# One reciprocal per pair in place of eight, four small GpSimd copies, and a new written order of the work

## The chip, the cores and the metric

The kernel runs on one core of a Trainium2 chip. A core has five engines with queues of their own: TensorE (PE in the profile, with its weight loads listed apart as PEld), VectorE (DVE), ScalarE (ACT), GpSimd (POOL) and SyncE (SP), which here issues all DMAs. PE writes only into PSUM; the other engines work on SBUF and, but for GpSimd, on PSUM too. The metric is the device time of one execution in microseconds, the median of several.

## The reference

Soft-capped attention over 8 batches, 12 heads, 448 positions and a head width of 64, followed by a feed-forward part whose gate comes from a causal convolution of 5 taps:

```python
scores = scale * np.matmul(q, k.transpose(0, 1, 3, 2))
scores = cap * np.tanh(scores / cap)
scores = scores - np.max(scores, axis=-1, keepdims=True)
attn = np.exp(scores)
attn = attn / (np.sum(attn, axis=-1, keepdims=True) + 1e-09)
attn_out = np.matmul(attn, v)                      # then (B, S, H * D), 768 wide
gate_pre += conv_w[k][None, None, :] * xp[:, k:k + S, :]   # for each of 5 taps
gate = 1.0 / (1.0 + np.exp(-gate_pre))
val = x @ w_val
return (gate * val @ w_out).astype(np.float32)
```

The step that the change touches is the division by the sum of each row of `attn`.

## The kernel before, in words

Two heads make a pair; there are 48 pairs, six to a batch. The 128 partitions hold the two heads' 64 channels each, as four groups of 32 partitions (`GROUPS`): groups 0 and 1 belong to the first head, groups 2 and 3 to the second. For a pair:

- SP loads q, k (four DMAs each) and v (two DMAs). DVE turns q and k in 32x32 blocks (L448). From pair 13 on, both are also cut into a high part (ACT, L454) and a low part (DVE, L383), and the scores are three products in place of one.
- PE makes the scores in four chunks of 112 keys (`scores`, L469) into one of two PSUM tiles (`pss`). ACT applies tanh (L477) and exp (L481) to each chunk (`pt`). DVE adds chunks together ahead of the row sums (`add`, L488 and L491): none for the first six pairs, all four into one from pair 11 on.
- PE multiplies `pt` with v into `psa` (`av`, L507) and with ones into `psz` (`sums`, L523). There is one buffer of each; the odd ones of the first six pairs use tiles named `psf` instead.
- Now the division. The sums of 448 rows are spread over the two groups of a head, 224 to a group. `turn_sums` (L529, DVE) turns them so that each partition has 7 sums, `norm_recip` adds the guard (L536) and takes reciprocals (L540), `spread` (L546, DVE) turns them back, now broadcast over 32 channels, and `norm_mul` (L554, DVE) multiplies `psa` by them into `u`. Every group needs the reciprocals of both halves of its head: its own 7 columns and those of the neighbour group. So L540 writes `rc`, 14 columns wide, with eight instructions of 32 partitions by 7 elements, half of which read from the neighbour's partitions.
- `u` is cut into `xh` (ACT, L559) and `xl` (DVE, L383) for the value projection, and DVE makes the convolution from it (L573, L575; the first tap of the first 11 pairs on ACT, L571).

For a batch, once its six pairs are there: ACT's sigmoid on the gates (L581), PE's value projection in halves of three channel blocks (`val`, L596 to L598, three products each), DVE's product with the gate (`gate`, L602), a high and a low part (`gated_hi` L605 on ACT, `gated_lo` L383 on DVE), PE's output projection in halves (`out_part`, L625 to L627), a copy out of PSUM (`store`, L633, ACT) and the DMA out (`store_out`, L637, SP). 448 is three and a half times 128, so every second batch leaves 64 rows to the next one: `keep_tail` (L612) moves them on GpSimd, twice for each of four batches. It is all that GpSimd does after the start. The two weight matrices are loaded and cut into high and low parts in twelve steps early on (L279 to L290), the convolution's weights once (`load_conv_w`; L300 loads, L311 to L314 prepare).

The order is written out by hand, as numbers. `PAIRS` has a row for each pair and in it a time for each step named in `STEPS`, counted in pairs and relative to the pair's own number; `BLOCKS` has a row for each batch, `WEIGHTS` for each weight step, and `CW_LOAD`, `CW_AT` and `W_FREE` place three single steps. All steps are sorted by these times and issued in that order under a manual schedule, so that each engine's queue, SP's and POOL's too, runs its instructions in exactly that order. An instruction whose input isn't there holds up all that stands behind it on its engine.

Of the kernel before, what the change touches and what calls it, by code (L numbers as in the profile page):

```python
# [7 lines left out]
F32 = mybir.dt.float32  # L8
# [34 lines left out]
    "add add add av av av av sums sums sums sums turn_sums recip spread mul x_hi x_lo conv conv conv conv conv"  # L43
).split()
PAIRS = """
- - -3.064 -9.09 -5.622 - - - - -4.262 -5.451 -4.05 -3.713 -3.983 -4.666 -3.924 -3.438 -3.329 -3.464 -3.153 -1.811 - -
  - -2.746 -2.598 -1.455 -0.365 -2.81 -1.83 -1.743 -1.539 -1.354 -1.021 0.536 0.696 1.014 3.151 1.192 1.24 1.616 1.869
  2.29
-5.242 -4.446 -1.697 -5.062 -4.398 - - - - -4.347 -4.229 -2.87 -2.909 -4.283 -3.621 -2.153 -2.144 -2.433 -1.59 -0.767
  -1.588 - - - -1.585 -1.248 -0.673 -0.458 -2.299 -1.473 0.346 0.383 0.475 0.582 0.646 0.669 2.05 2.71 1.397 2.009  # L50
  2.138 2.228 2.305
-4.37 -4.577 -1.599 -3.197 -3.579 - - - - -2.956 -1.738 -1.485 -0.821 -2.404 -1.055 -0.603 -0.573 -1.126 -0.649 -0.165
  -0.246 - - - -0.498 -0.333 0.44 0.542 -1.035 -0.323 -0.032 0.045 0.622 0.651 0.927 1.346 2.559 2.796 1.643 2.115
  2.477 2.536 2.862
-3.867 -3.827 -0.48 -3.708 -2.408 - - - - -1.417 -1.284 -1.129 -0.899 -1.259 -1.006 -0.603 -0.517 -0.987 -0.577 -0.121
  0.182 - - - -0.092 0.457 0.74 0.839 -0.67 -0.089 0.042 0.439 0.522 0.625 0.709 1.033 2.962 3.062 1.339 1.695 1.805
  2.076 2.385
-2.147 -3.045 -0.082 -1.922 -2.656 - - - - -1.37 -0.682 -0.02 -0.433 -0.576 -0.258 0.044 -0.177 -0.16 -0.144 0.242
  0.055 - - - 0.076 0.114 0.466 0.498 0.048 0.332 0.425 0.434 0.742 0.82 0.952 1.348 2.039 2.351 1.815 2.116 2.374
  2.436 2.515  # L60
-3.132 -2.604 -0.301 -2.118 -1.544 - - - - -0.68 -1.014 -0.654 -0.433 -0.544 -0.823 -0.138 0.222 -0.286 -0.093 0.036
  0.269 - - - 0.255 0.453 0.668 0.75 -0.24 0.21 0.414 0.553 0.669 0.722 0.984 1.101 1.256 1.566 1.471 1.551 2.023
  2.457 2.71
-2.592 -2.549 -0.928 -1.311 -1.58 - - - - -0.222 -0.561 -0.183 -0.988 -0.182 -0.397 -0.049 -0.65 0.08 0.167 0.202
  0.211 0.4 0.521 - 0.179 0.224 0.335 0.872 0.799 0.872 - - 1.024 1.233 1.519 1.751 3.543 3.796 2.13 2.869 3.058 3.256
  3.886
-2.49 -2.096 -0.928 -1.564 -1.888 - - - - -0.119 -0.898 -0.11 -0.988 0.3 -0.435 0.536 -0.422 0.429 0.505 0.667 0.745
  1.102 1.056 - 0.977 1.043 1.054 1.08 1.147 1.202 - - 1.219 1.38 1.485 1.753 2.392 3.921 3.14 3.64 3.787 3.931 3.989
-1.946 -2.927 -0.201 -1.477 -0.909 - - - - -0.199 -0.174 0.359 0.264 -0.126 0.044 0.638 0.423 0.708 0.35 0.717 0.797
  0.977 1.023 - 0.829 0.854 1.048 1.269 1.087 1.236 - - 1.679 1.752 1.784 1.986 2.393 3.269 2.657 3.368 3.424 3.498  # L70
  3.653
-2.393 -2.701 0.359 -1.57 -0.973 - - - - -0.338 -0.119 -0.33 0.024 -0.277 0.072 -0.018 0.087 0.751 0.714 0.556 0.552
  1.063 1.24 - 1.227 1.274 1.404 1.425 1.191 1.395 - - 1.65 1.803 1.982 2.063 2.96 3.19 2.44 3.241 3.241 3.314 3.627
-2.751 -1.165 0.435 -1.245 -0.761 - - - - -0.701 0.069 -0.683 0.143 -0.014 0.329 -0.498 0.452 0.245 0.622 0.789 0.934
  0.958 1.087 - 1.201 1.226 1.26 1.341 1.097 1.272 - - 1.329 1.533 1.662 1.704 2.377 2.856 2.579 2.733 2.863 2.916
  3.42
-1.653 -2.409 -0.503 -1.187 -1.793 - - - - 0.056 -0.489 -0.487 0.07 0.532 -0.335 -0.192 0.27 0.641 0.818 -0.083 0.684
  1.055 0.816 1.111 0.78 0.867 1.056 1.058 1.114 - - - 1.202 1.273 1.71 1.757 1.778 1.858 2.275 2.63 2.65 3.045 3.412
-1.985 -2.388 -0.519 -0.474 -0.538 - - - - -0.444 -0.458 0.268 0.163 -0.013 -0.095 0.589 0.356 0.179 0.681 0.882 0.927
  1.039 1.099 1.326 1.055 1.366 1.425 1.426 1.507 - - - 1.517 1.633 1.782 1.782 2.76 3.615 1.902 2.302 2.801 2.812  # L80
  3.214
-3.454 -1.521 0.862 -1.941 -0.941 -1.662 -0.798 -0.758 -0.355 0.036 0.039 0.529 0.517 0.293 0.286 0.589 0.573 0.359
  0.306 0.619 0.752 0.577 0.79 0.852 1.078 1.094 1.161 1.481 1.255 - - - 1.375 1.407 1.527 1.762 2.714 2.89 2.216
  2.427 2.707 3.284 3.378
# [36 lines left out]
-2.966 -2.807 0.096 -2.131 -1.597 -0.618 -1.292 -0.287 -0.879 -0.107 -0.061 0.233 0.37 -0.039 0.069 0.627 0.493 0.099
  0.33 0.636 0.502 0.408 0.71 0.809 0.909 0.986 1.146 1.366 0.819 - - - 1.134 1.166 1.458 1.653 2.3 2.369 2.503 2.552
# [739 lines left out]
```

## Time and profile before

| | |
|---|---|
| median of 3 runs | 733.51 us (733.31 to 734.77) |
| profiled execution | 733.1 us |
| its span, first to last instruction | 731.2 us |
| PE busy | 699.2 us (96%) |
| DVE busy | 622.2 us (85%) |
| ACT busy | 593.3 us (81%) |
| POOL busy | 7.1 us (1%) |
| mean granted TensorE clock | 0.997 |

How to read the rows that follow. A group of instructions is "line engine operation out<-in, shapes, xcount | busy us, mean ns of one | us that its engine idled ahead of it, and what ended the idle time". A row of waits is "engine tile line <- what it waited for: us in all, times, longest". A row of a timeline is "start us, us, engine line operation out<-in, xcount", with idle time ahead and what ended it in brackets; neighbouring instructions of one kind are merged into a row. A row of stages is "from:to, length, busy us of each engine, granted clock (1.00 is full), share of the DMA engines, GB/s".

### The profile page before, as it was taken

What the parts mean: (1) busy time and instruction counts of PE and PEld (TensorE: products, weight loads), DVE (VectorE), ACT (ScalarE), POOL (GpSimd) and SP (SyncE); (2) the same over time, 40 slices, a digit from 0 to 9 for tenths busy, and PEclk for the clock granted to TensorE, in tenths of its full rate; (3) what the DMA queues carried; (4) which work ended last, traced back from release to release, by engine and by line L of the source; (5) the groups of instructions that cost most, each with busy time, mean ns of one, the idle gap of its engine ahead of it and who ended that gap; (6) DMA issues with size and microseconds to landing.
All of it is one profiled execution on the core that took longest, in us unless ns stands there. A gap on an engine that the chain in (4) does not pass through costs nothing.

```text
span 731.2 us, 13364 instructions
## 1 busy us (share of the span) xinstructions
PE 699.2 (96%) x5024; PEld 480.1 (66%) x5024; DVE 622.2 (85%) x1308; ACT 593.3 (81%) x750; POOL 7.1 (1%) x16
## 2 busy tenths in 40 slices
PE   4899999999999999999999999999999999999997
PEld 1233465656766876676676677667675777666997
DVE  2599999999999988999899988899888888998620
ACT  5799989978898989879897889887987889986211
POOL 0000000000000000000000000000000000010000
PEclk9999999999999999999999999999999999999999
DMA  7887779843234422343132442126402442101001
GB/s 148 177 231 166 157 199 233 197 120 69 46 60 110 89 45 60 63 84 66 22 75 53 93 85 60 31 45 126 82 3 58 92 91 49 37 13 56 12 24 67
DMA packets 241830, 63.89 MB, mean 87 GB/s; under 512 B 228448, under 2 KB 235616, under 8 KB 241760
## 3 DMA queue, kind: packets, MB, share of 16 engines
q1 hardware_dynamic: 241760, 62.98, 38.9%
q8 instruction: 41, 0.67, 0.4%
q14 instruction: 29, 0.24, 0.1%
HBM read 51.94 MB, written 11.01 MB: 86 GB/s over the span
## 4 chain that ended last, share of the span: by engine, by line
PE 39%; DVE 26%; ACT 10%; issue 3%; DMA 2%; SPq 1%; DVEq 0%; ACTq 0%
PE psa L507 8%; PE pss L469 6%; DVE gate L575 5%; DVE pa L491 5%; PE psf L625 4%; PE psf L627 4%; PE psf L626 4%; ACT pt L481 4%; PE psf L596 3%; PE psf L598 3%; PE psf L597 3%; DVE rc L540 3%; ACT pt L477 2%; DVE pa L488 2%; ACT L481 1%
## 5 line engine op out<-in xcount | busy, mean ns | idle before, releaser
L477 ACT ACTIVATE pt<-pss,rc 112x896 f32<-112x896 f32 x192 | 188.7, 1003 | 51.3 <-PE pss L469 49.6
L481 ACT ACTIVATE pt<-pt,capt 112x896 f32<-112x896 f32 x192 | 194.9, 1042 | 1.3
L507 PE MATMUL psa<-pt,vn 112*32 112x448 f32 x1440 | 152.0, 544 | 2.1 <-DVE u L554 1.7
L575 DVE SCALAR_TENSOR_TENSOR gate<-u,cw,gate 128x448 f32<-128x448 f32 x192 | 127.5, 672 | 1.3
L625 PE MATMUL psf<-wo,g_h 128*128 128x384 f32 x336 | 115.5, 344 | 0.0
L627 PE MATMUL psf<-wo,g_l 128*128 128x384 f32 x336 | 112.9, 336 | 1.7 <-DVE g_l L383 1.6
L626 PE MATMUL psf<-wo,g_h 128*128 128x384 f32 x336 | 112.6, 335 | 0.0
L596 PE MATMUL psf<-xh,wv 128*128 128x448 f32 x288 | 108.2, 376 | 4.4 <-DVE gate L602 2.0
L491 DVE TENSOR_TENSOR pa<-pt 112x896 f32<-112x896 f32 x84 | 90.7, 1089 | 19.9 <-ACT pt L481 19.2
L598 PE MATMUL psf<-xl,wv 128*128 128x448 f32 x288 | 106.1, 369 | 0.7 <-DVE xl L383 0.6
L597 PE MATMUL psf<-xh,wv 128*128 128x448 f32 x288 | 105.8, 368 | 0.0
L507 PEld LDWEIGHTS psa<-pt,vn 112*32 112x32 f32 x1440 | 43.3, 110 | 73.2 <-issue 53.6
L540 DVE RECIPROCAL rc<-zc 32x7 f32<-32x7 f32 x384 | 73.8, 192 | 6.6
L625 PEld LDWEIGHTS psf<-wo,g_h 128*128 128x128 f32 x336 | 63.0, 188 | 11.2 <-issue 9.2
L596 PEld LDWEIGHTS psf<-xh,wv 128*128 128x128 f32 x288 | 54.0, 188 | 18.1 <-issue 5.8
L627 PEld LDWEIGHTS psf<-wo,g_l 128*128 128x128 f32 x336 | 63.1, 188 | 2.7 <-DVE g_l L383 2.6
L626 PEld LDWEIGHTS psf<-wo,g_h 128*128 128x128 f32 x336 | 63.1, 188 | 0.3 <-DVE wo L290 0.3
L469 PE MATMUL pss<-qt,kt 64*112 64x448 f32 x208 | 50.8, 592 | 10.6 <-DVE guard L392 7.9
L598 PEld LDWEIGHTS psf<-xl,wv 128*128 128x128 f32 x288 | 54.0, 188 | 6.8 <-DVE xl L383 1.7
L469 PE MATMUL pss<-qh,kh 64*112 64x448 f32 x280 | 58.2, 411 | 0.0
L597 PEld LDWEIGHTS psf<-xh,wv 128*128 128x128 f32 x288 | 54.1, 188 | 4.6
L469 PE MATMUL pss<-ql,kh 64*112 64x448 f32 x280 | 51.6, 363 | 0.1
(74 smaller groups left out, 854.2 us busy)
## 6 DMA issues: line engine op xcount, KB each, us to landing
vn<-in_v_dram SPq DMA_DIRECT2D x96, 112.0 KB, 2.7
out_dram<-osb SPq DMA_DIRECT2D x56, 192.0 KB, 2.3
qn<-in_q_dram SPq DMA_DIRECT2D x188, 56.0 KB, 2.5
kn<-in_k_dram SPq DMA_DIRECT2D x188, 56.0 KB, 2.5
w_raw<-in_moe_w_val_dram SPq DMA_DIRECT2D x12, 384.0 KB, 4.0
w_late<-in_moe_w_val_dram SPq DMA_DIRECT2D x12, 384.0 KB, 4.2
w_raw<-in_moe_w_out_dram SPq DMA_DIRECT2D x12, 384.0 KB, 3.9
w_late<-in_moe_w_out_dram SPq DMA_DIRECT2D x12, 384.0 KB, 4.7
```

Source lines behind the costliest of these rows:

```text
L469: nc.tensor.matmul(ps[:CH, j, :S], st[x][r, c], st[y][r], start=(n == 0), stop=(n == len(parts) - 1))
L477: nc.scalar.activation(st["p", i], st.pop(("s", i)), AF.Tanh, scale=rc8[:CH])
L481: nc.scalar.activation(t, t, AF.Exp, scale=capt[:CH])
L491: nc.vector.tensor_tensor(st["a", i], st["p", 2 * i], st["p", 2 * i + 1], op=ALU.add)
L507: nc.tensor.matmul(st["o"][r, :S], vloads[p][:, j, i, d:d + BLK], t[:, j], start=(i == 0), stop=(i == NKT - 1))
L575: nc.vector.scalar_tensor_tensor(g, u[:, i:i + S], cw[:, hp, i:i + 1], g, ALU.mult, ALU.add)
L596: nc.tensor.matmul(o, w_h, xh, start=(c == 0), stop=False)
L597: nc.tensor.matmul(o, w_l, xh, start=False, stop=False)
L598: nc.tensor.matmul(o, w_h, xl, start=False, stop=(c == NCC - 1))
L625: nc.tensor.matmul(o, g_h[:, d, s], w_h, start=(d == 0), stop=False)
L626: nc.tensor.matmul(o, g_h[:, d, s], w_l, start=False, stop=False)
L627: nc.tensor.matmul(o, g_l[:, d, s], w_h, start=False, stop=(d == NCC - 1))
```

## The change

`norm_recip` takes one reciprocal over all 128 partitions. Its input is the 7 sums of each partition, read twice by a broadcast, so that both halves of a row of `rc` (now 2 x 7) hold the partition's own reciprocals. One half of each row is right and the other belongs to the neighbour group. A new step, `shift`, puts that right with four GpSimd copies of 32 partitions by 7 elements, two for each head. `spread` reads the same 14 columns as before.

```diff
@@ norm_recip
-            rc = wk.tile([P, S // BLK], F32, name="rc", bufs=1)
+            rc = wk.tile([P, D // BLK, HC], F32, name="rc", bufs=1)
             zc = wk.tile([P, HC], F32, name="zc", bufs=1)
             col = st["zt"].rearrange("p (c e) -> p c e", e=BLK)[:, :HC, 0]
             nc.vector.tensor_scalar(zc, col, guard, None, ALU.add)
-            for g, r in enumerate(GROUPS):
-                j, d = divmod(g * BLK, D)
-                for x in range(D // BLK):
-                    nc.vector.reciprocal(rc[r, x * HC:(x + 1) * HC], zc[GROUPS[j * D // BLK + x]])
+            nc.vector.reciprocal(rc, zc.unsqueeze(1).to_broadcast([P, D // BLK, HC]))
             st["rc"] = rc
 
+        def shift(p):
+            rc = state[p]["rc"]
+            for g in range(0, P // BLK, 2):
+                nc.gpsimd.tensor_copy(rc[GROUPS[g], 1], rc[GROUPS[g + 1], 1])
+                nc.gpsimd.tensor_copy(rc[GROUPS[g + 1], 0], rc[GROUPS[g], 0])
+
         def spread(p):
             st = state[p]
-            rc = st.pop("rc").unsqueeze(2).to_broadcast([P, S // BLK, BLK])
+            rc = st.pop("rc").rearrange("p x c -> p (x c)").unsqueeze(2).to_broadcast([P, S // BLK, BLK])
             nc.vector.transpose(st["zt"].rearrange("p (c e) -> p c e", e=BLK), rc)
```

`STEPS` gets a `shift` between `recip` and `spread`, and every number of the order's tables is another. The tables still hold the same steps for each pair and batch (the same adds, sums and loads), the new `shift` apart. In the first pairs, for one, these loads stand on SP's queue up to the convolution's weights:

```diff
-weight 0, q 1, k 1, v 0, k 2, late part of weight 0, q 2, q 3, k 3, v 1, weight 1, convolution's weights
+k 1, q 1, weight 0, v 0, q 2, late part of weight 0, k 2, v 1, weight 1, convolution's weights
```

and single steps are placed anew:

```diff
-CW_LOAD, CW_AT, W_FREE = -0.325, 0.739, 11.226
+CW_LOAD, CW_AT, W_FREE = -0.238, 0.0592, 11.5281
```

More of the change, by code (lines that the diff above doesn't have):

```diff
@@ L42 @@
     "load_q load_k load_v tq tk q_hi k_hi q_lo k_lo scores scores scores scores tanh tanh tanh tanh exp exp exp exp "
-    "add add add av av av av sums sums sums sums turn_sums recip spread mul x_hi x_lo conv conv conv conv conv"
+    "add add add av av av av sums sums sums sums turn_sums recip shift spread mul x_hi x_lo conv conv conv conv conv"
 ).split()
 PAIRS = """
-- - -3.064 -9.09 -5.622 - - - - -4.262 -5.451 -4.05 -3.713 -3.983 -4.666 -3.924 -3.438 -3.329 -3.464 -3.153 -1.811 - -
-  - -2.746 -2.598 -1.455 -0.365 -2.81 -1.83 -1.743 -1.539 -1.354 -1.021 0.536 0.696 1.014 3.151 1.192 1.24 1.616 1.869
-  2.29
@@ L49 @@
[L49 to L60, printed above, removed]
@@ L181 @@
[L181 to L186 removed]
+- - -4.3452 -12.1786 -10.8774 - - - - -9.9955 -5.8528 -4.3155 -3.9585 -4.8825 -4.2355 -4.0746 -3.4896 -4.304 -3.6763
+  -3.6674 -2.7702 - - - -2.7595 -1.4891 -1.2888 0.0359 -4.22 -3.609 -2.4641 -1.6265 -0.7193 -0.4462 -0.1116 -0.0078
+  0.7465 1.648 3.076 1.1925 1.8515 1.8829 2.2003 3.0551
@@ new lines @@
+-7.5913 -9.9254 -2.1232 -4.2974 -5.4213 - - - - -4.2767 -3.9218 -2.0116 -3.0691 -3.5919 -2.07 -1.2483 -1.9478 -3.3023
+  -1.3442 -1.1707 -1.4419 - - - -0.4848 -0.2665 0.123 0.362 -2.629 -0.8907 -0.4577 -0.085 0.2491 0.5353 0.9703 1.1046
+  1.1999 1.9634 2.3322 1.2365 1.5883 1.8833 2.0343 2.3129
+-6.154 -3.8379 -0.0392 -3.2165 -2.8234 - - - - -2.5406 -2.147 -1.4484 -1.2283 -2.2457 -1.6644 -0.8625 -0.3907 -0.9039
+  -1.2531 -0.5922 -0.0815 - - - 0.3095 0.3494 0.6253 0.935 -0.4524 -0.198 0.2582 0.2889 0.397 0.8188 1.0723 1.2929
+  1.3197 2.061 3.0337 1.4955 1.5861 2.2123 2.3092 2.4336
@@ new lines @@
+-2.1341 -2.229 -0.2285 -1.634 -1.7644 - - - - -1.1341 -1.1414 -0.915 -0.8322 -0.9113 -1.0741 -0.2516 -0.3357 -0.6511
+  0.0302 0.022 0.12 - - - 0.4787 0.5161 0.572 0.8184 -0.2 0.1751 0.3062 0.4768 0.4873 0.7142 1.2064 1.2527 1.7501
+  2.8166 2.9704 2.2085 2.6863 2.9237 2.9973 3.0941
+-1.7792 -1.728 -0.4065 -1.7633 -1.2023 - - - - -0.8562 -0.825 -0.3963 -0.4916 -0.8465 -0.7428 -0.0036 -0.3595 -0.7409
+  -0.6383 0.1087 0.3298 - - - 0.0454 0.061 0.6077 0.8003 -0.4569 -0.2292 0.2551 0.6956 0.9828 1.0192 1.3196 1.3493
+  1.3648 2.0638 2.1828 2.1942 2.2222 2.9449 3.0753 3.0965
@@ new lines @@
+-1.7203 -1.6592 -0.5366 -1.3983 -1.2291 - - - - -1.1229 -1.0013 -0.3427 -0.3216 -0.7395 -0.8094 -0.1027 -0.1486
+  -0.6183 -0.3565 0.0133 -0.0769 - - - 0.2815 0.2932 0.3332 0.5656 -0.2936 -0.266 0.0382 0.2043 0.5098 0.711 0.9313
+  1.0776 1.225 1.3255 1.5794 1.93 2.0718 2.4645 2.5679 3.199
+-2.1424 -1.9971 -0.6088 -1.4746 -1.5048 - - - - -1.0481 -1.0241 -0.4443 -0.6372 -0.6727 -0.7025 -0.1345 -0.136 -0.1482
+  -0.4481 0.0133 -0.0193 0.0048 0.1033 - -0.0271 0.0826 0.2245 0.256 0.2095 0.3337 - - 0.3881 0.4793 0.4853 0.7668
+  1.1225 1.8695 3.2102 1.1617 2.2362 2.7661 3.1808 3.2728
@@ new lines @@
+-2.0472 -2.3254 -0.403 -1.1075 -1.2624 - - - - -1.0574 -1.0953 -0.4796 -0.6006 -0.9451 -0.9359 -0.3497 -0.4198 0.1313
+  -0.5275 0.2286 0.3721 0.3593 0.6082 - 0.2378 0.2784 0.9167 0.9221 0.6905 0.8035 - - 0.9864 1.0994 1.1508 1.2555
+  1.5491 2.2588 3.2537 2.4177 2.7205 3.4214 3.6042 3.6453
+-2.139 -1.6247 -0.804 -1.5582 -1.2365 - - - - -1.1898 -0.7002 -1.0665 -0.3607 -0.9274 -0.5027 -0.6347 -0.2691 -0.5743
+  0.2387 0.0699 -0.2195 0.5853 0.2167 - 0.6217 0.6438 0.7586 0.8446 0.7192 0.75 - - 0.7814 1.0782 1.1487 1.2397 1.2796
+  1.6005 2.695 1.7587 1.7685 3.0519 3.1746 3.3252
@@ new lines @@
+-1.8633 -2.5637 -0.7438 -1.6049 -1.5113 - - - - -1.0557 -1.0533 -0.4838 -0.4359 -0.9826 -0.653 -0.2841 -0.1514 -0.2964
+  -0.3424 0.5004 0.1282 0.479 0.8969 - 0.7059 0.9578 1.0613 1.2706 0.7439 1.1744 - - 1.2658 1.2727 1.3279 1.6136
+  1.6891 2.528 3.623 2.1852 2.2772 2.6602 3.5047 3.6902
+-2.3121 -2.2477 -0.3495 -2.0902 -1.7895 - - - - -0.8515 -0.372 -0.8199 -0.2964 -0.763 -0.1389 -0.5296 0.4956 -0.0424
+  0.5027 -0.1918 0.6706 0.6754 0.7125 - 0.9378 0.9767 1.0198 1.0412 1.0051 1.119 - - 1.3016 1.3081 1.4245 1.6932
+  1.8569 2.5732 2.7586 2.0351 2.9424 3.1903 3.3699 3.5469
@@ new lines @@
+-2.3379 -2.0726 -0.187 -2.0582 -1.066 - - - - -0.228 -0.459 -0.4738 -0.2368 0.1499 -0.3415 -0.3475 0.093 0.563 -0.2733
+  0.1095 0.2301 1.0853 1.0757 1.3048 0.9682 1.1549 1.2767 1.3042 1.3448 - - - 1.4166 1.499 1.6415 1.7176 1.8343 1.8413
+  1.9062 2.203 2.2823 2.5401 2.6077 3.0503
+-2.0523 -2.5786 -0.2419 -1.1637 -1.0981 - - - - -0.1214 -0.247 -0.6078 -0.8773 0.657 0.3938 -0.3773 -0.7839 0.8518
+  0.4529 -0.3331 -0.7418 1.0756 0.3361 1.1765 1.0979 1.1294 1.236 1.3442 1.2965 - - - 1.2978 1.3442 1.514 1.5252
+  1.7265 1.8839 3.1317 1.9361 2.0688 2.3318 2.356 3.174
@@ new lines @@
+-3.2335 -2.2192 0.1005 -1.9778 -1.1134 -1.343 -0.9385 -1.3017 -0.4149 -0.1164 0.1784 0.6248 0.5348 0.4719 0.2701
+  0.7499 0.75 0.5474 0.3625 1.0957 0.8712 0.9853 1.2189 1.2367 1.1526 1.2022 1.2097 1.3293 1.2937 - - - 1.6112 1.6419
+  1.6632 1.7869 1.9546 2.6191 3.8395 2.8605 3.4479 3.495 3.5156 3.5331
+-1.653 -3.2938 0.9378 -1.3831 -1.6957 -1.2531 -1.1497 -0.3903 -0.8933 0.0869 -0.0137 0.51 0.4312 0.4624 0.4046 0.801
+  0.6069 0.581 0.5023 0.94 0.8152 0.9628 1.0911 1.107 1.0039 1.0676 1.1021 1.2288 1.1196 - - - 1.2103 1.4313 1.6565
+  1.7442 1.8476 2.646 3.526 2.1306 2.2515 2.4991 2.6624 3.9586
@@ L230 @@
-5.665 6.331 6.649 6.814 6.902
-7.22 7.504 7.321 7.492 7.601
-7.753 7.872 7.92 8.212 8.258
-8.38 9.002 8.596 8.955 9.003
-9.003 9.417 9.139 9.39 9.752
-9.629 9.957 10.028 10.439 10.522
-10.814 10.823 11.017 11.163 11.196
+-4.5948 -4.0529 -1.2373 -1.205 -0.9113
+-0.954 0.464 -0.0342 0.3861 1.223
+1.201 2.7582 2.1899 2.2079 3.4612
+3.3115 3.8319 3.9692 4.0726 4.3848
+4.2645 4.7528 5.3306 5.7667 5.7945
+5.8432 6.2447 6.2222 6.3475 6.7468
+6.4785 6.8341 6.9323 7.0955 7.2314
+7.2209 7.3558 7.4711 7.736 7.8402
@@ L237 @@
+7.7627 8.354 8.3229 8.5 8.5929
+8.8442 8.9584 9.2184 9.4551 9.7041
+10.0273 10.3227 10.3569 10.4117 10.4774
+10.5154 10.5835 10.7963 10.8681 11.0407
 """
-CW_LOAD, CW_AT, W_FREE = -0.325, 0.739, 11.226
+CW_LOAD, CW_AT, W_FREE = -0.238, 0.0592, 11.5281
 NPAIRED, NPLAIN = 11, 13
@@ L653, in fast_path @@
             q_lo=lambda p: half_lo("q", p), k_lo=lambda p: half_lo("k", p),
-            scores=scores, tanh=tanh, exp=exp, add=add, av=attnv, sums=sums, turn_sums=turn_sums, recip=norm_recip,
+            scores=scores, tanh=tanh, exp=exp, add=add, av=attnv, sums=sums, turn_sums=turn_sums, recip=norm_recip, shift=shift,
             spread=spread, mul=norm_mul, x_hi=x_hi, x_lo=x_lo, conv=conv,
```

230 lines of the change are left out of this document (99 added, 131 removed), and 68 rows, old and new, of the table BLOCKS.

## The prediction

> **What bounds the kernel now.** I read the page's engine totals and chain of waits first, then busy time by stage, then the groups by line, and last the timelines at the places where TensorE (PE) stops.
>
> ```profile
> span 731.2 us, 13364 instructions
> PE 699.2 (96%) x5024; PEld 480.1 (66%) x5024; DVE 622.2 (85%) x1308; ACT 593.3 (81%) x750; POOL 7.1 (1%) x16
> PE 39%; DVE 26%; ACT 10%; issue 3%; DMA 2%; SPq 1%; DVEq 0%; ACTq 0%
> ```
>
> PE is the bound: 96% busy, with 731.2 - 699.2 = 32.0 us idle. The chain that ended last still runs through VectorE (DVE) for 26% and ScalarE (ACT) for 10%: those are the places where PE and its feeders are about level. Where the 32 us lie is told by four stages (head, weights still being prepared, steady state, tail):
>
> ```profile
> core 0: us, PE busy (x) PEld busy (x) DVE busy (x) ACT busy (x) POOL busy (x), PEclk, DMA share, GB/s
> 0.00:65.00 65.00, 50.56 (x392) 16.70 (x396) 42.66 (x105) 50.78 (x61) 0.64 (x8) 0.97 0.81 179
> 65.00:175.00 110.00, 105.39 (x734) 63.21 (x727) 106.41 (x222) 98.04 (x123) 1.46 (x2) 1.00 0.70 169
> 175.00:680.00 505.00, 496.17 (x3658) 355.30 (x3657) 460.92 (x963) 433.87 (x549) 5.03 (x6) 1.00 0.30 63
> 680.00:731.20 51.20, 47.08 (x252) 44.87 (x250) 12.18 (x21) 10.65 (x21) 0.00 (x0) 0.99 0.11 36
> ```
>
> PE idle by stage is 14.4, 4.6, 8.8 and 4.1 us. The 4.1 us at the end are the last store, and the first matmul waits 7.9 us for its inputs; neither is touched:
>
> ```profile
> PE pss L469 <- DVE guard L392: 7.9, 1, 7.9
> ```
>
>  What any change of feeders can win by idle time is 14.4 - 7.9 = 6.5 us in the head and 4.6 + 8.8 = 13.4 us from 65 to 680 us, plus matmuls slowed by a lower clock. In those 615 us DVE is busy (106.41 + 460.92) / 615 = 92% and ACT (98.04 + 433.87) / 615 = 86%.
>
> **The reciprocals.**
>
> ```profile
> L540 DVE RECIPROCAL rc<-zc 32x7 f32<-32x7 f32 x384 | 73.8, 192 | 6.6
> L386 DVE RECIPROCAL rc<-capt 128x1 f32<-128x1 f32 x1 | 0.2, 164 | 0.7 <-DVE small L826 0.7
> 23.39 1.63 DVE L540 RECIPROCAL rc<-zc 32x7 f32<-32x7 f32 x8
> ```
>
> Eight instructions of a pair take 1.63 us from first to last; 48 pairs make 78 us of DVE's line. The new one covers 128 partitions by 14 elements, which the trace does not show. By the two sizes there, 6 more elements cost 192 - 164 = 28 ns, so 14 cost about 192 + 7 x 28/6 = 225 ns. From below it is one 32x7 (192 ns), from above eight of them back to back (1.63 us), if the work went by rows. I take 0.23 us, because 128 rows at one element cost no more than 32 rows at seven. Saved: 1.40 us a pair, 67 us over 48; bounds 0 to 1.44 a pair.
>
> **The four copies.** No row has a GpSimd copy of 32x7 from one group of partitions to another. Rows near it:
>
> ```profile
> L394 POOL MEMSET ones<- 128x32 f32 x1 | 0.1, 124 | 4.0 <-DVE small L826 4.0
> L311 POOL COPY cw_m<-cw_raw 128x60 uint16<-128x60 uint16 x1 | 0.2, 234 | 27.7 <-DMA cw_raw<-in_moe_conv_w_dram 27.7
> L612 POOL TENSOR_SCALAR g_l<-g_l 128x384 fp32r<-128x384 f32 x4 | 3.3, 827 | 1.2 <-DVE g_l L383 1.2
> ```
>
> Bounds 0.12 and 0.83 us; I take 0.23, since seven elements are nearer to the copy of 60 than to the 384. Four make 0.9 us on an engine that is 1% busy. The chain of a pair gets 1.40 shorter by the reciprocal and 0.9 us longer by the copies, with two handoffs that no row prices; I bound them by 0 and by the 0.65 us of the idle before the second POOL row below. So the chain is about level, while DVE's line is shorter: this is where the stall goes, into spread (L546), which waits for POOL with DVE's queue behind it. In the new table at least two other DVE steps stand between recip and spread in 38 of 48 pairs (0.62 to 1.08 us each by the five DVE rows of the next part, so 1.2 us of cover and more); in ten pairs there are none or one. If that cover were gone everywhere, spread would wait 0.9 us and more, still less than the 1.40 saved. Nothing of the removal is lost to the wait alone.
>
> POOL is in order, and keep_tail is its other work. In the new table the shift of pair 45 is POOL's next work behind the keep_tail of batch 6, whose last low half is made just before it; batches 0 and 4 have a shift close behind too. Such a shift waits out two POOL instructions, and spread and u with it. I put 0.7 us on PE at two places, 1.4 us; bounds 0 and 2.6 a place (0.83 + 1.78, the longest POOL instruction below).
>
> **The shared way into SBUF.** Around 645 us the trace has both engines:
>
> ```profile
> 645.09 0.52 POOL L612 TENSOR_SCALAR g_h<-g_h 128x384 fp32r<-128x384 f32 x1 [171.18 <-PE pss L469]
> 646.26 1.78 POOL L612 TENSOR_SCALAR g_l<-g_l 128x384 fp32r<-128x384 f32 x1 [0.65 <-DVE g_l L383]
> ```
>
> ```profile
> 644.62 0.62 DVE L554 TENSOR_TENSOR u<-psa,zt 128x448 f32<-128x448 f32 x1
> 645.15 0.93 DVE L383 TENSOR_TENSOR g_l<-gate,g_h 128x448 fp32r<-128x448 f32 x1
> 646.00 1.08 DVE L491 TENSOR_TENSOR pa<-pt 112x896 f32<-112x896 f32 x1
> 647.00 0.67 DVE L575 SCALAR_TENSOR_TENSOR gate<-u,cw,gate 128x448 f32<-128x448 f32 x1
> 647.60 1.39 DVE L491 TENSOR_TENSOR pa<-pt 112x896 f32<-112x896 f32 x1
> ```
>
> A DVE instruction with two SBUF operands that starts 0.06 us into a POOL instruction takes 0.93 us in place of some 0.62; and the second POOL instruction takes 1.78 in place of 0.52 us, because two DVE instructions pass it first. A copy of 0.23 us can therefore cost DVE between nothing and 0.23 us, and itself be late by one or two DVE instructions. I take 0.07 us per copy, 0.3 a pair, which leaves DVE 1.1 us a pair, 53 us in all. The Trainium skill, "SBUF — State Buffer", section "SBUF: two separate sides", goes further: the pair of ports is an exclusive lock held for the whole instruction, and the other side is fully blocked. By it all of 4 x 0.23 us would go off DVE's gain in every pair; that is the first rival below. The trace agrees in kind, but DVE resumed earlier than POOL's recorded end: 645.15 + 0.93 - 0.62 = 645.46, against 645.61.
>
> **The new order.** The counts in the tables stay: as many matmuls, adds, sums and DMAs, and of PE's changes from one kind of step to another 303 before and 304 after. One count does change. ACT reloads its table whenever sigmoid alternates with tanh or exp:
>
> ```profile
> L581 ACT ACT_TABLE_LOAD x29 | 37.2, 1283 | 0.4
> L481 ACT ACT_TABLE_LOAD x28 | 35.9, 1283 | 0.5
> L391 ACT ACT_TABLE_LOAD x1 | 1.3, 1283 | 4.4 <-DVE small L826 4.4
> ```
>
> The old table gives 58 such changes, as the rows do; the new one, counted the same way, 46. Twelve at 1.283 us take 15.4 us off ACT.
>
> The second difference is in the head, on SP's queue:
>
> ```profile
> 23.83 1.01 SPq L338 DMA_DIRECT2D vn<-in_v_dram x2
> 25.89 4.07 SPq L300 DMA_DIRECT2D cw_raw<-in_moe_conv_w_dram x5
> ```
>
> and what waited for them, with the clock that PE was then granted (columns as in the stages above):
>
> ```profile
> 26.79 2.21 PE L507 MATMUL psf<-pt,vn 112*32 112x448 f32 x8 [2.39 <-DMA vn<-in_v_dram]
> ...
> 32.32 0.23 ACT L279 ACTIVATE cw_t<-cw_raw 128x30 f32<-128x30 f32 x1 [5.22 <-DMA cw_raw<-in_moe_conv_w_dram]
> ```
>
> ```profile
> 27.00:30.40 3.40, 3.40 (x26) 1.46 (x26) 0.00 (x0) 0.10 (x1) 0.00 (x0) 0.50 0.93 207
> ```
>
> PE idles 2.39 us for pair 1's v and then runs 3.40 us at half clock (1.7 us lost), while ACT idles 5.22 us for the convolution's weights. In the new order q and k of pair 3 no longer stand ahead of these loads:
>
> ```profile
> 15.97 4.60 SPq L326 DMA_DIRECT2D qn<-in_q_dram x8
> 20.67 3.12 SPq L326 DMA_DIRECT2D kn<-in_k_dram x4
> ```
>
> Half of the first row and the whole of the second, 2.30 + 3.12 = 5.4 us of queue, are gone from in front: more than either wait. What is late next is pair 3's q and k; their scores come after pair 2's 8 ACT instructions, about 8 us. I take the whole stall, 2.4 + 1.7 = 4.1 us; bounds 0 and 4.1 + (6.5 - 2.4) = 8.2.
>
> **Steady state.** DVE's busy time between 65 and 680 us falls by 1.1 x 44 pairs = 48 us (44 of the 48 are divided after 65 us), from 92% to 84%; ACT's by some 15, from 86% to 84%. Of the 13.4 us I take 40%, 5.4: DVE's own idle time roughly doubles (8% to 16%), which should halve the waits that come of its queue, and not the others. Bounds 0 and 13.4. **The sum:** 733.1 us, the profiled execution (span 731.2 and 1.9 around it; 0.4 below the median of the runs, 733.51), less 4.1 and 5.4, plus 1.4: 725.0.
>
> **Rivals.**
>
> *The copies hold DVE up.* DVE loses 4 x 0.23 = 0.9 us a pair, is left with 0.5, and the steady-state gain shrinks in that ratio, 5.4 x 0.5 / 1.1 = 2.5: 728 us. For it the 0.93 us above; against it that a copy must fall on a two-operand instruction each time. Chance 0.12.
>
> *Starved copies: slower.* Place: spread, then u (L554), then the next pair's first attention matmul, since psa has one buffer.
>
> ```profile
> PEld psa L507 <- DVE u L554: 5.6, 10, 1.4
> ```
>
> Ten such waits are there now. In the new order the shortest stretch of PE work between a pair's sums and the next use of psa is four score steps, half a val step and half an out step. Of this the DVE chain after sums without copies needs about 2.1 us (0.41 + 0.22 + 0.23 + 0.64 + 0.62 by its rows):
>
> ```profile
> L529 DVE STREAM_TRANSPOSE zt<-psz 128x224 f32<-128x224 f32 x45 | 18.2, 405 | 5.4 <-PE psz L523 5.0
> L536 DVE TENSOR_SCALAR zc<-zt,guard 128x7 f32<-128x7 f32 x48 | 10.7, 222 | 0.6
> L546 DVE STREAM_TRANSPOSE zt<-rc 128x448 f32<-128x448 f32 x48 | 30.6, 637 | 0.3
> L554 DVE TENSOR_TENSOR u<-psa,zt 128x448 f32<-128x448 f32 x45 | 27.7, 615 | 5.6 <-PE psa L507 4.2
> ```
>
> It decides from the point where the copies take longer than the 1.40 us saved, that is when two of four each wait out an add of 1.08 us. With one more such add and copy (1.08 + 0.23 = 1.3) on ten pairs PE loses 13 us: 733.1 - 9.5 + 13 = 736.6, about 737. For it the 1.78 us row; against it that DVE does useful work meanwhile. Chance 0.14.
>
> *Nothing reaches PE.* It is 96% busy; the waits that go are replaced by others of the new order: 733. Chance 0.14.
>
> *More than that.* All 13.4 us less a fifth, 10.7, and in the head half of the further 4.1, 2.1: 733.1 - 4.1 - 10.7 - 2.1 + 1.4 = 717.6. Chance 0.12.
>
> *The reciprocal is not cheaper.* The one wide instruction takes the 1.63 us of the eight, and the copies come on top; the head's 4.1 and a quarter of 5.4 by ACT stay, less 1.4 for keep_tail and 1.4 for longer chains: 733.1 - 4.1 - 1.4 + 2.8 = 730.4. Chance 0.06.
>
> **How the numbers follow.** The forecast, 725.0, has 0.42, with a range of its own of 721 to 729. The range 717 to 735 takes in "more" and "nothing" and leaves out most of "slower" and the far ends. About 0.2%, 1.5 us, is what a measurement can tell here from no change: faster 0.42 + 0.12 + 0.12 + 0.06 = 0.72, same 0.14, slower 0.14.
>
> **What would show it.** Right: 48 wide reciprocals near 0.23 us; POOL copies under 0.3 us; 46 table loads; DVE's total near 570 us; no wait for vn or cw_raw of over a microsecond before 35 us and no half clock there; PE's total within 1% of 699 with less idle from 65 to 680. Wrong: spread waiting for POOL for over 40 us in all; copies over 0.8 us, or reciprocals near 1.6; PE idle moved to another wait of the head, such as pair 3's q and k; more idle before psa.

## The result

| | before | after |
|---|---|---|
| median | 733.74 us (733.31 to 734.77, 4 runs) | 710.25 us (710.02 to 711.57, 4 runs) |
| profiled execution | 733.1 us | 710.17 us |
| its span | 731.2 us | 708.3 us |

After stands to before as 0.9682 (95% interval 0.9665 to 0.9698): 23 us faster, where the forecast was 8 us and its range ended at 717. The head of the page of after:

```profile
span 708.3 us, 13291 instructions
PE 689.1 (97%) x5024; PEld 481.2 (68%) x5024; DVE 557.7 (79%) x972; ACT 576.5 (81%) x738; POOL 76.6 (11%) x208
PE 85%; ACT 9%; SPq 2%; DVE 1%; DMA 1%; issue 1%; ACTq 0%
```

DVE's share of the chain that ended last fell from 26% to 1%; PE's rose from 39% to 85%. PE's own busy time fell by 10.1 us with the same 5024 matmuls, while its weight loads stayed (480.1 and 481.2 us). So the "busy" PE time of before held time in which nothing was gained; 1.7 us of it are the matmuls at half clock that the prediction shows for 27.0 to 30.4 us.

Stages of equal time can't be compared when one kernel runs ahead of the other. I cut both at equal numbers of matmuls instead (the columns are those of the prediction's stages; the counts match within 4). Before:

```profile
0.00:70.10 70.10, 55.66 (x444) 18.41 (x448) 47.60 (x120) 55.85 (x67) 0.64 (x8) 0.98 0.81 179
70.10:186.60 116.50, 111.89 (x771) 69.22 (x763) 112.03 (x229) 104.28 (x129) 1.46 (x2) 1.00 0.67 160
186.60:683.40 496.80, 487.97 (x3585) 350.69 (x3584) 453.57 (x946) 425.11 (x541) 5.03 (x6) 1.00 0.30 63
```

After:

```profile
0.00:65.00 65.00, 51.33 (x440) 17.86 (x440) 40.58 (x84) 56.18 (x66) 6.75 (x27) 1.00 0.90 183
65.00:175.00 110.00, 109.55 (x768) 69.64 (x767) 103.38 (x178) 104.76 (x132) 15.47 (x36) 1.00 0.78 177
175.00:660.00 485.00, 484.52 (x3586) 351.92 (x3585) 402.47 (x692) 407.33 (x526) 54.39 (x146) 1.00 0.31 63
```

The gain of a stage is the difference of the two lengths; the part that was PE idle is the difference of length less PE busy, and the rest was counted as busy before. The two orders place the matmuls around these ends differently, so a stage's figure is good to about half a microsecond.

| stage | gain, us | from PE idle | from PE "busy" |
|---|---|---|---|
| head | 70.1 - 65.0 = 5.1 | 14.44 - 13.67 = 0.8 | 55.66 - 51.33 = 4.3 |
| weights prepared | 116.5 - 110.0 = 6.5 | 4.61 - 0.45 = 4.2 | 2.3 |
| steady state | 496.8 - 485.0 = 11.8 | 8.83 - 0.48 = 8.4 | 3.4 |
| tail (what is left of the span) | 47.8 - 48.3 = -0.5 | | |

They sum to 22.9 us, the difference of the spans. Behind the head PE of after is idle for 0.9 us in 595. The view that tells why is what PE itself waited for. Before, from 65 to 680 us (columns: us in all, times, longest):

```profile
PE psz L523 <- DVE pa L488: 3.8, 5, 1.1
PE psf L596 <- DVE gate L602: 2.0, 2, 1.2
PE psf L596 <- DVE u L554: 1.7, 1, 1.7
PE psa L507 <- DVE u L554: 1.7, 3, 1.0
PE psf L627 <- DVE g_l L383: 1.6, 2, 1.0
PE psz L523 <- DVE pa L491: 0.7, 2, 0.4
PE psf L596 <- ACT osb L633: 0.6, 1, 0.6
PE psf L598 <- DVE xl L383: 0.6, 1, 0.6
```

After, from 65 to 660 us, all of it:

```profile
PE psf L530 <- ACT pt L488: 0.4, 1, 0.4
PE psf L638 <- DVE g_l L390: 0.2, 1, 0.2
PE psz L530 <- DVE pa L495: 0.2, 1, 0.2
```

Of the 12.7 us of before, 12.1 were ended by DVE, and by five different lines of it: both adds for the sums, the gate's product, `u`, low parts. So no one step of a pair stands out as the late one; that it was DVE's line as a whole is what the experiments test.

The operations themselves, after (groups by line; the number after the bar is busy us, then mean ns; behind the second bar the idle time ahead):

```profile
L544 DVE RECIPROCAL rc<-zc 128x14 f32<-128x14 f32 x48 | 11.6, 242 | 1.6
L551 POOL COPY rc<-rc 32x7 f32<-32x7 f32 x96 | 33.2, 346 | 555.2 <-DVE rc L544 553.2
L552 POOL COPY rc<-rc 32x7 f32<-32x7 f32 x96 | 35.4, 369 | 3.9
L557 DVE STREAM_TRANSPOSE zt<-rc 128x448 f32<-128x448 f32 x48 | 30.7, 639 | 11.6 <-POOL rc L552 11.0
L592 ACT ACT_TABLE_LOAD x23 | 29.5, 1283 | 0.4
L488 ACT ACT_TABLE_LOAD x22 | 28.2, 1283 | 0.4
L398 ACT ACT_TABLE_LOAD x1 | 1.3, 1283 | 4.4 <-DVE small L837 4.4
```

### The profile page after: what moved, and what is told of

The parts are those of the page before. It is cut to its first block, busy times and chain, and to the rows that moved or that the text cites. A ratio compares the mean times of both kernels' runs of the same rounds, so it can differ in the third digit from the quotient of the medians.

```text
span 708.3 us, 13291 instructions
## 1 busy us (share of the span) xinstructions
PE 689.1 (97%) x5024; PEld 481.2 (68%) x5024; DVE 557.7 (79%) x972; ACT 576.5 (81%) x738; POOL 76.6 (11%) x208
## 4 chain that ended last, share of the span: by engine, by line
PE 85%; ACT 9%; SPq 2%; DVE 1%; DMA 1%; issue 1%; ACTq 0%
PE psa L514 17%; PE pss L476 16%; PE psf L607 9%; PE psf L636 8%; PE psf L608 8%; PE psf L609 8%; PE psf L638 8%; PE psf L637 8%; ACT pt L484 3%; ACT pt L488 3%; PE psz L530 2%; SPq L333 1%; ACT L488 1%; DMA qn<-in_q_dram 1%; SPq L307 1%
## 5 line engine op out<-in xcount | busy, mean ns | idle before, releaser
L514 PE MATMUL psa<-pt,vn 112*32 112x448 f32 x1440 | 150.3, 542 | 0.0
L586 DVE SCALAR_TENSOR_TENSOR gate<-u,cw,gate 128x448 f32<-128x448 f32 x192 | 125.6, 663 | 1.0 <-ACT gate L582 0.2
L551 POOL COPY rc<-rc 32x7 f32<-32x7 f32 x96 | 33.2, 346 | 555.2 <-DVE rc L544 553.2
L636 PEld LDWEIGHTS psf<-wo,g_h 128*128 128x128 f32 x336 | 63.0, 188 | 10.1 <-issue 7.5
L644 ACT COPY osb<-psf 128x384 f32<-128x384 f32 x56 | 26.5, 477 | 45.6 <-PE psf L638 44.2
```

The costliest lines, as they stand in the source:

```text
L514: nc.tensor.matmul(st["o"][r, :S], vloads[p][:, j, i, d:d + BLK], t[:, j], start=(i == 0), stop=(i == NKT - 1))
L586: nc.vector.scalar_tensor_tensor(g, u[:, i:i + S], cw[:, hp, i:i + 1], g, ALU.mult, ALU.add)
L636: nc.tensor.matmul(o, g_h[:, d, s], w_h, start=(d == 0), stop=False)
```

## The experiments

Each time is a median, each ratio is to the kernel before on the same chip, with its 95% interval. Differences between two kernels are differences of their ratios times 733.7 us. The diffs below show the new lines: where a run swaps the operation, the lines of the other one go, and `spread` reads `rc` as the new one lays it out.

### The new operation and the new order, one at a time

The old tables with the wide reciprocal, and the four copies straight behind it:

```diff
 (norm_recip, order of before)
+            nc.vector.reciprocal(rc, zc.unsqueeze(1).to_broadcast([P, D // BLK, HC]))
+            for g in range(0, P // BLK, 2):
+                nc.gpsimd.tensor_copy(rc[GROUPS[g], 1], rc[GROUPS[g + 1], 1])
+                nc.gpsimd.tensor_copy(rc[GROUPS[g + 1], 0], rc[GROUPS[g], 0])
```

> The order of before, with the one wide reciprocal and the four copies; each pair's copies follow its reciprocal at once on POOL. Theory A (VectorE's line was what held PE up in the steady state, and any lighter VectorE frees it): the head keeps its stall, so of the 23 us some 4 stay away, and most of the rest comes: 715 to 720 us. Theory B (the new order as such, with its fewer table loads and its placing, did it): 728 to 734 us.

Measured: 719.83 us, 0.9802 (0.9781 to 0.9823), as theory A has it.

The new tables with the eight reciprocals, and a `shift` that does nothing:

```diff
 (norm_recip and shift, order of after)
+            for g, r in enumerate(GROUPS):
+                j, d = divmod(g * BLK, D)
+                for x in range(D // BLK):
+                    nc.vector.reciprocal(rc[r, x * HC:(x + 1) * HC], zc[GROUPS[j * D // BLK + x]])
...
         def shift(p):
+            pass
```

> The order of after, with the eight small reciprocals of before at the place of the one, and no copies. Theory A: VectorE is as loaded as before, so only the head's 4 us and a little of the table loads are kept: 724 to 730 us. Theory B: 710 to 715 us.

Measured: 733.82 us, 1.000 (0.9981 to 1.002), outside the ranges of both theories: not even the head's 4 us came. The operation alone brings 14.5 us, the order alone nothing, both 23.3. So they don't add: the order brings about 9 us, but only on a DVE line that is light enough. With eight reciprocals in the new order PE waits for the same kind of line as before (first three rows of PE's waits, 65 to 680 us):

```profile
PE psa L514 <- DVE u L564: 4.9, 6, 1.1
PE psf L637 <- DVE g_l L390: 3.1, 4, 2.0
PE psz L530 <- DVE pa L495: 2.4, 5, 0.8
```

Where the order's part lies is told by the stages of the old order with the new operation, cut at the same matmuls:

```profile
0.00:69.10 69.10, 54.11 (x444) 17.91 (x448) 42.53 (x88) 56.12 (x67) 4.81 (x28) 1.00 0.85 182
69.10:180.80 111.70, 110.58 (x771) 69.65 (x764) 101.53 (x173) 103.66 (x129) 12.42 (x32) 1.00 0.69 166
180.80:670.50 489.70, 485.76 (x3586) 351.72 (x3585) 405.79 (x698) 425.14 (x541) 44.13 (x148) 1.00 0.30 63
```

Against after's 65.0, 110.0 and 485.0 the order is worth 4.1 us in the head, 1.7 while weights are prepared and 4.7 in the steady state (10.5 us between the two profiles, about 9 by the ratios).

One difference between these two kernels lies in the copies themselves. In the old order none or one other DVE instruction stands between the reciprocal and `spread` in 21 of 48 pairs, in the new one in 10, and `spread` waits 22.7 us for the copies in all, against 11.0 in after. Some of the order's 9 us may be this cover. No run of the old order leaves the copies out, so that rival stays open.

### What the copies cost

After without them; half of the reciprocals in each row then belong to the wrong group, which is the part of the computation left out:

```diff
         def shift(p):
-            rc = state[p]["rc"]
-            for g in range(0, P // BLK, 2):
-                nc.gpsimd.tensor_copy(rc[GROUPS[g], 1], rc[GROUPS[g + 1], 1])
-                nc.gpsimd.tensor_copy(rc[GROUPS[g + 1], 0], rc[GROUPS[g], 0])
+            pass
```

> After without the four copies: half of each row's reciprocals stay those of the wrong group, everything else is as it is. If the copies cost PE time (spread waits 11.0 us for them in all, and they hold VectorE up): 704 to 708 us. If they are hidden: within 1 us of 710.2.

Measured: 710.05 us, 0.9666 (0.9645 to 0.9688), not told apart from after: they are hidden. DVE is busy 556.0 us without them and 557.7 with them:

```profile
PE 689.1 (97%) x5024; PEld 481.5 (68%) x5024; DVE 556.0 (78%) x972; ACT 576.2 (81%) x738; POOL 7.0 (1%) x16
```

So the copies cost the kernel nothing that can be measured. Many are late, though: half of them take about 0.19 us, the longest 1.71. At 270 us of after one sees how (start us, us, instruction), first POOL and then DVE:

```profile
270.34 0.20 POOL L551 COPY rc<-rc 32x7 f32<-32x7 f32 x1 [12.44 <-DVE rc L544]
270.58 1.71 POOL L552 COPY rc<-rc 32x7 f32<-32x7 f32 x1
272.33 0.19 POOL L551 COPY rc<-rc 32x7 f32<-32x7 f32 x1
```

```profile
270.56 1.09 DVE L498 TENSOR_TENSOR pa<-pt 112x896 f32<-112x896 f32 x1
271.57 0.68 DVE L586 SCALAR_TENSOR_TENSOR gate<-u,cw,gate 128x448 f32<-128x448 f32 x1
272.16 0.62 DVE L613 TENSOR_TENSOR gate<-psf,gate 128x448 f32<-128x448 f32 x1
```

The second copy ends at 272.29, just behind the second of two DVE instructions with two SBUF inputs (271.57 + 0.68 = 272.25); the third runs in 0.19 us beside an instruction whose other input, `psf`, is in PSUM. So the copy waited for DVE here. In the other direction, of all DVE instructions that overlapped a copy I find one that took longer than its kind, by 0.04 us.

### How heavy may DVE's line be

Two kernels put work back into the new order, without touching its results: seven, or three, throwaway reciprocals behind `norm_mul` of every pair (the lines show the first; the second has `range(3)`).

```diff
 (norm_mul, order of after)
+            junk = wk.tile([P, HC], F32, name="junk", bufs=1)
+            for n in range(7):
+                r = GROUPS[n % len(GROUPS)]
+                nc.vector.reciprocal(junk[r], ones[r, :HC])
```

> After with seven more reciprocals of 32x7 per pair on VectorE, into a tile that nobody reads, directly behind norm_mul: VectorE's line is as long as before the change, but the pair's own way from the sums to u is as short as after it. If it is the occupied line that held PE up: 728 to 735 us, as with the eight reciprocals in their place (733.8). If it is the time from the sums to u of the same pair: 711 to 716 us.

> The same with three of them, 0.6 us per pair on VectorE. If the time follows VectorE's line in proportion: 710.3 plus 3/7 of what the seven cost, about 719 to 721 us if those cost 23. If there is room for a part of it and a point beyond which it costs: under 715 us.

Measured: seven, 743.29 us, 1.0123 (1.0098 to 1.0149); three, 717.91 us, 0.9779 (0.9754 to 0.9804). Three cost 7 us and seven 32. Neither time lies in a range that was given: seven cost 8 us more than the largest, and three fall between the two. With seven, PE waits for DVE's adds again (the first two rows of PE's waits, 65 to 670 us):

```profile
PE psz L530 <- DVE pa L495: 14.5, 16, 1.5
PE psf L642 <- DVE g_l L390: 3.8, 2, 2.6
```

DVE's total there, 617.7 us, is close to that of the new order with the old operation (620.4), which is 9 us faster. So where the work stands on DVE's line matters beside how much it is.

Three more take work away. Two leave out the third and fourth tap of the convolution, which are DVE work off the path from sums to `u`, one in before and one in after; the computation lacks those two taps:

```diff
 (conv)
+            if i in (2, 3):
+                return
```

> The kernel before without the third and the fourth tap of the convolution (left out for all 48 pairs): 96 instructions of 0.67 us, 64 us less on VectorE, as much as the new operation takes off, but on the way to the gate and not from the sums to u; the eight reciprocals stay. If the length of VectorE's line is what counts: 718 to 722 us, as the old order with the new operation. If the pair's own way from sums to u counts: 728 to 733 us.

> After without the same two taps: another 64 us less on VectorE. If VectorE no longer holds PE up after the change: 708 to 710.5 us. If it still does in the same measure: 697 to 704 us.

The last keeps the old order, and writes the wrong half of each row by four small reciprocals on DVE in place of the copies, five instructions in place of eight:

```diff
 (norm_recip, order of before)
+            nc.vector.reciprocal(rc, zc.unsqueeze(1).to_broadcast([P, D // BLK, HC]))
+            for g in range(0, P // BLK, 2):
+                nc.vector.reciprocal(rc[GROUPS[g], 1], zc[GROUPS[g + 1]])
+                nc.vector.reciprocal(rc[GROUPS[g + 1], 0], zc[GROUPS[g]])
```

> The old order with five reciprocals per pair in place of eight, no copies: one of 128x14, then four of 32x7 that overwrite the neighbour's halves. About 0.6 us less per pair on VectorE, 30 us in all, 0.45 of what the change takes off. If the time falls in proportion: 733.7 - 0.45 x 13.9 = about 727.5 us. If the first microseconds taken off bring the most, as the curve of added work suggests (the last four cost 26 us, the first three 7): 722 to 725 us.

With the DVE totals of their pages:

| kernel | DVE busy, us | median, us | ratio |
|---|---|---|---|
| old order, eight reciprocals (before) | 622.2 | 733.74 | 1 |
| old order, five reciprocals | 597.3 | 722.78 | 0.9855 (0.9835 to 0.9874) |
| old order, eight, two taps less | 567.6 | 722.84 | 0.9843 (0.9824 to 0.9863) |
| old order, one reciprocal and copies | 558.8 | 719.83 | 0.9802 (0.9781 to 0.9823) |
| new order, eight reciprocals | 620.4 | 733.82 | 1.000 (0.9981 to 1.002) |
| new order, one, and three throwaway | 581.8 | 717.91 | 0.9779 (0.9754 to 0.9804) |
| new order, one (after) | 557.7 | 710.25 | 0.9682 (0.9665 to 0.9698) |
| new order, one, two taps less | 502.4 | 710.54 | 0.9680 (0.9661 to 0.9699) |

The two taps take 55 us off DVE's total and not the 64 that were expected, and before without them is 0.8 us beyond the nearer range. The five reciprocals came as their second case had it, and after without the taps as its first, to a tenth.

Two things follow. Taking taps away, which takes no work off a pair's path to `u`, brings 11.5 us in the old order: the length of DVE's line counts in its own right. That the place of the work adds nothing is not shown: 25 us less on that path bring nearly as much (10.6 us) as 55 us less elsewhere. And the gain is bent: in the old order the first 25 us off DVE bring 10.6 us, the next 38 some 4 more, though there the copies' 22.7 us of waiting come in; in the new order, where only the taps go, the 55 us below 558 bring nothing. Its steady stage is then the same to 0.02 us of PE:

```profile
175.00:660.00 485.00, 484.54 (x3587) 352.59 (x3586) 361.21 (x622) 407.23 (x526) 48.79 (x146) 1.00 0.31 63
```

### Are the order's 9 us its table loads?

The order has 46 table loads and before 58. A first run put six lone sigmoids among the exps of after, which makes 58 again:

```diff
 (exp, order of after)
+            if i == 0 and p in (10, 16, 22, 28, 34, 40):
+                nc.scalar.activation(lone, lone, AF.Sigmoid)
```

> After, with six lone sigmoids of one element per partition ahead of the first exp of pairs 10, 16, 22, 28, 34 and 40, so that ScalarE loads its table 58 times, as before, and not 46: 15.4 us more on ScalarE, nothing else moved. If the table loads that fell away were a main part of the gain: 716 to 722 us. If ScalarE has room there: 710 to 712 us.

Measured: 716.48 us, 0.9756 (0.9735 to 0.9777), 5.4 us slower than after and in the range for the loads. From this I took the loads for most of the order's part. That theory predicts that the old order gains as much when its own loads go from 58 to 46, which six sigmoids moved next to others do, with the new operation and without:

```diff
+MOVED = {(2, 0): 18.94389, (2, 2): 18.9441, (3, 1): 24.91889, (4, 5): 32.76789, (6, 1): 42.1321, (6, 2): 42.1322}
...
-                at(t0 + next(row), sigmoid, b, d)
+                when = t0 + next(row)
+                at(MOVED.get((b, d), when), sigmoid, b, d)
```

> The old order with the new operation (as the first experiment), and six sigmoids moved up to others of their batch, so that ScalarE loads its table 46 times and not 58. If the parts add up once VectorE is light (6.2 us for twelve loads, as the lone sigmoids cost): 713 to 716 us. If the old order has no use for it: 719 to 720 us.

> The kernel before with the same six sigmoids moved, eight reciprocals as they were: 15.4 us off ScalarE alone. If VectorE's line decides while it is long, so that a lighter ScalarE brings nothing: 732 to 735 us. If ScalarE held PE up in its own right, and the new order ran no faster with the old operation only because it was planned for another one: 726 to 729 us.

Measured: with the new operation 719.20 us, 0.9793 (0.9777 to 0.9809), not told apart from 0.9802; without it 732.97 us, 0.9983 (0.9973 to 0.9993), 1.2 us. In the same way, after with 36 and with 30 loads:

> After with six sigmoids moved likewise, 36 table loads, 12.8 us less on ScalarE. If ScalarE still holds PE up: 705 to 708 us. If PE has next to nothing left to win outside the head: 709 to 711 us.

> After with ten sigmoids moved, some close ahead of the gate product that needs them, 30 table loads, 20.5 us less on ScalarE. As for 36 loads, or worse by waits of VectorE's gate for ScalarE: 705 to 712 us.

Measured: 710.15 us, 0.9670 (0.9654 to 0.9686), and 709.03 us, 0.9659 (0.9642 to 0.9675); neither is told apart from after. The theory fell. Taking away loads that the kernel has brings 0.7 to 1.7 us in these four kernels, and only the 1.2 us of before are told from nothing; loads that are added at places for which the order made no room cost 5.4. With them PE waits for the copy out of PSUM, which stands behind them on ACT:

```profile
PE psf L641 <- ACT osb L649: 4.1, 3, 1.7
```

### The head

After with pair 3's q and k once more ahead of pair 1's v, of weight step 1 and of the convolution's weights on SP's queue:

```diff
 (PAIRS, row 3: times of its q and k)
--2.1341 -2.229 ...
+-4.3 -4.2 ...
```

> After with q and k of pair 3 loaded ahead of v of pair 1, weight step 1 and the convolution's weights, as before the change; two loads are moved on SP's queue, nothing else. If these places were what the head gained, the waits come back (2.4 us of PE for v, 5.2 us of ScalarE for the convolution's weights): 713 to 716 us. If the head's gain has another cause: within 1 us of 710.3.

Measured: 713.07 us, 0.9714 (0.9689 to 0.9739), 2.3 us slower than after, with intervals that overlap, though all four of its runs are above all four of after. ACT waits for the convolution's weights again and DVE's wait behind it grows from 2.9 us to 5.5, but the stall in front of pair 1's `av` is not back. PE waits elsewhere, 2.72 us for a tanh that stands behind these weights on ACT:

```profile
DVE cw_t L290 <- ACT cw_t L286: 5.5, 1, 5.5
ACT cw_t L286 <- DMA cw_raw<-in_moe_conv_w_dram: 1.3, 1, 1.3
33.79 1.04 PE L476 MATMUL pss<-qt,kt 64*112 64x448 f32 x4 [2.72 <-ACT pt L484]
```

Its first 65 us hold 428 matmuls in place of 440, at a clock of 0.97:

```profile
0.00:65.00 65.00, 50.07 (x428) 17.34 (x432) 39.40 (x82) 53.79 (x63) 6.90 (x24) 0.97 0.84 179
```

That clock can't be put down to these loads. The kernel with the lone sigmoids has after's order in the head, with as many matmuls there, and:

```profile
0.00:65.00 65.00, 53.15 (x440) 18.25 (x440) 40.55 (x84) 56.06 (x66) 7.48 (x27) 0.97 0.89 184
```

Last, since DVE of after has room, the first taps of pairs 0 to 5 were moved from ACT to DVE:

```diff
 (conv)
-            if i == 0 and p < NPAIRED:
+            if i == 0 and NPAIR <= p < NPAIRED:
```

> After with the convolution's first tap of pairs 0 to 5 on VectorE in place of ScalarE: ScalarE, which has no gap from 9.8 to 40 us, gets 6 x 0.66 = 4.0 us less in the first 70 us, VectorE 6 x 0.44 = 2.6 us more. If ScalarE paces the head: 707 to 709 us. If not: 710 us or a little more.

Measured: 711.15 us, 0.9678 (0.9652 to 0.9704): no difference from after. No kernel tried is clearly faster than after.

## Why the prediction was right or wrong

**The direction** was right, and the change does what it says. **The steady-state term was wrong**, and with it the time. The step that failed is "Of the 13.4 us I take 40%, 5.4: DVE's own idle time roughly doubles (8% to 16%), which should halve the waits that come of its queue, and not the others." From the end of the head on, the gain was 6.5 + 11.8 = 18.3 us. The forecast 5.4 us were thus 12.9 short. The order is not all of that: with the new operation alone these two stages gained 4.8 + 7.1 = 11.9 us. The step failed in two ways:

- *The share.* There were hardly any others: 12.1 of PE's 12.7 us of waits were ended by DVE. The prediction shows one row of that kind, for `psa`, and took a share of the idle time without asking who ended the rest. And they weren't halved. With a tenth less work on DVE they fell to 0.4 us in after, the last two rows of its three being DVE's. The runs that lighten DVE in the old order show the bend: the first 25 us bring most of the gain.
- *The bound.* "What any change of feeders can win by idle time is 14.4 - 7.9 = 6.5 us in the head and 4.6 + 8.8 = 13.4 us from 65 to 680 us, plus matmuls slowed by a lower clock." I then let no case in the steady state go beyond it, and the range ended at 717. Of the 18.3 us, 12.5 were idle time and 5.8 were counted as busy. Matmuls overlap and their ends are modelled, so a short wait between two of them may lie inside busy time; that this is what the 5.8 us were is not shown, only that the same matmuls and weight loads took that much less. The Trainium skill, "Perfetto Trace Analysis", section "Identifying the Most-Contended Engine", says that matmul busy time isn't a good measure of how near a kernel is to its limit; the 10.1 us that PE's busy time lost with no matmul taken away (1.7 of them the half clock of the head) agree with it. That section's reason is that pipelined instructions look smaller in a trace, and no run here shows whether that is what happened.

**Part and order.** The prediction summed the head's order, the lighter DVE and ACT's loads as if each stood alone. The order alone is worth nothing and on the light line about 9 us. The lighter DVE alone gives 719 to 720 us, inside the range. What of the order makes its 9 us is open but for some 2.3 us of the head; it isn't the table loads. Better cover for the copies is one candidate that no run tests; which of the moves bring the rest was not found.

**The head**: 4.1 us foreseen, 5.1 measured, but not for the reasons given. PE's wait for pair 1's v and ACT's for the convolution's weights are gone, as foreseen. But PE's idle time there fell by 0.8 us and not by 2.4, since two new waits took the place of the one for v, ahead of pair 2's and of pair 3's scores in after:

```profile
24.91 2.11 PE L476 MATMUL pss<-qt,kt 64*112 64x448 f32 x8 [1.68 <-DVE kt L455]
36.85 1.76 PE L476 MATMUL pss<-qt,kt 64*112 64x448 f32 x8 [1.75 <-DVE zc L543]
```

That is a sign of being wrong that the prediction named, "PE idle moved to another wait of the head". The other 4.3 us of the gain were counted as busy. Of the 5.1 us, the old order with the new operation has 1.0 by itself, with a clock of 1.00 there. Putting the loads back in after costs 2.3, not 4.1, and the wait for v doesn't return with them. The 1.7 us for the half clock was no property of the order: the profiles of before and of the kernel with after's head (0.97) show such a stretch, that of after doesn't, and after's own four runs have mean clocks from 0.996 to 1.000. The Trainium skill, "TensorE: Matmul & The Clock Gate", section "Part 1: The HAM clock gate (the "warmup" mystery)", says that the clock's window runs freely and that the same kernel may meet it differently from run to run; the 1.00 and 0.97 for the same head agree with it, though no run here shows the window.

**The reciprocal**: 0.23 us foreseen, 0.242 measured. The rival in which it is not cheaper is out.

**The copies**: 0.23 us foreseen; 0.346 and 0.369 on the mean, about 0.19 when nothing is in the way. That a copy may be "late by one or two DVE instructions" is right (the 1.71 us above). "0.07 us per copy" off DVE was wrong: DVE's total is 1.7 us larger with the copies, 0.01 us for each, which is why DVE's total is 557.7 us and not near 570 (192 x 0.07 = 13.4). So the rival *The copies hold DVE up* has no ground here. The rule that the prediction cites for it, from the Trainium skill, "SBUF — State Buffer", section "SBUF: two separate sides", by which whichever of the two sides comes first blocks the other for its whole instruction, shows for these copies only in one direction: GpSimd waits for DVE. The 0.93 us of before, from which I had it, came beside a GpSimd instruction of 128x384; these are 32x7.

**The stall moved into spread**, as foreseen, 11.0 us in 48 pairs and not the 40 us that would have told against the forecast; the longest wait was 1.1 us. DVE had room for it: without copies the time is the same. The chain of a pair is "about level", as foreseen: from the start of `turn_sums` to the end of `norm_mul` I work out from the trace 7.25 us before and 7.02 after, on the mean. The 1.4 us for `keep_tail` did not appear: a shift that waited out two POOL instructions and held PE 0.7 us would be one of the waits of PE listed above, and there is none for `u`. *Starved copies: slower* asked for copies that wait out adds on ten pairs, with PE held before `psa`; PE has no such wait left from 65 to 660 us, and the ten waits of its weight loads there (5.6 us) became two (1.0 us).

**Table loads**: 46 as counted. That they bring next to nothing was not foreseen, though the term had no price of its own.

**The signs**: "PE's total within 1% of 699" failed, 689.1 being 1.4% less. It was the sign that idle time isn't the whole of what a feeder can win.

## What to carry to other kernels

Before taking a share of the bound engine's idle time, list its own waits by who ended them: where nearly all name one feeder, though by many different lines, that feeder's queue is probably too long as a whole; here a tenth off it removed nearly all of them. Don't take idle time as the upper bound of a gain on PE; compare stretches of equal matmul count. And a written order and the operations in it have one price together: the order paid only with the lighter operation, and once it had paid, work added at a place it had not planned for cost more (5.4 us for 15.4 us of loads) than taking the same kind of work away brought (1.7 us at most).

## What the runs showed of the hardware

- A GpSimd copy of 32x7 between neighbouring groups of 32 partitions took 0.18 to 0.19 us in half of 192 cases. Beside DVE instructions with two SBUF inputs it took up to 1.71 us, two of them in a row passing it. Of DVE's instructions beside a copy one was longer than its kind, by 0.04 us.
- DVE's reciprocal of 128x14 takes 242 ns where 32x7 takes 192: four times the partitions and twice the elements of each for a quarter more time.
- The same first 65 us ran at a granted clock of 1.00 in one kernel's profile and 0.97 in another's with the same head, so a half-clock stretch of some 3.4 us in one profile is no term for a sum.
